# Storing each output tile with one transfer, and splitting the last tile's buffers, in a gated-attention + MLP kernel

## The chip, the cores and the metric

The kernel runs on one core of a Trainium2 chip. The metric is device time of one execution in microseconds (us). In three runs it took 189.67, 190.49 and 190.68 us; the median is 190.49 us.

## The reference

Two parts follow one another. The first is a gated linear recurrence over 768 positions for 4 batches of 8 heads, with a head size of 48; the state of a head is a 48x48 matrix:

```python
for t in range(S):
    state = alpha[:, :, t, :, None] * state + einsum('bhd,bhe->bhde', k[:, :, t], v[:, :, t])
    y[:, :, t] = einsum('bhd,bhde->bhe', q[:, :, t], state)
```

The second takes the heads of a position side by side as a row of 384 numbers, so that x has 4 x 768 = 3072 rows, and runs a two-layer network over them, with w_in of 384x2048 and w_out of 2048x384:

```python
h = x @ w_in
g = h * cos(h)
return (g @ w_out).astype(float32)
```

The output has 3072 rows of 384 float32, 4.72 MB in all.

## The kernel before

**Tiles.** The positions are worked off in 12 groups J of 256 (three to a batch). A group is held as pairs: a partition holds an even and an odd position beside one another in the inputs, so that a load of one input for one group (`load`, L105) brings 128 partitions x 8 heads x 384 bytes, 384 KB, and the group's output rows come out in two tiles c = 0 and 1 of 128 rows.

**Stages of a group.** `mul_a` and `ln` take logarithms of alpha, `cums` sums them on TensorE (PE), `icp` and `exps` turn them into decay factors on ScalarE (ACT), `scale_k` and `scale_q` (L212, L216) apply these to k and q, mostly on GpSimd (POOL). `trans`, `scores`, `mask` and `outer` build the attention inside the group, `add_state` and `decay_state` carry the state. `stack_v` (L225) copies v within the on-chip memory (SBUF) with four transfers of 64 partitions x 1 KB into the tile `vs`, and `yT` (L340) needs `vs` for its second set of matmuls. Then come the two layers: `mlp1` (L359, w_in), `cosine` (L365), `gate` (L370), and `mlp2` (L387, w_out), which sums a tile of outputs over 16 matmuls in a single bank of the accumulation memory (PSUM), tag "o". `evict_o` (L396) copies that bank to one of four SBUF tiles `o_sb`, and `store` (L403) writes it to the output in DRAM.

**The last tile.** For group 11, c = 1, `mlp2` puts the two halves of 192 columns in the two banks of one PSUM tile `o_last` (L381), `evict_o` copies one half with ACT and the other with VectorE (DVE) into the two halves of one `o_sb` tile (L394), and `store` writes each half with two transfers.

**Stores.** Row 2i+e of a tile's 128 output rows lies in partition 64e+i. `store` therefore writes the even and the odd rows with a transfer each: 64 partitions x 1536 bytes, to 64 rows that are 3072 bytes apart.

**Order.** It is written out by hand: `PLAN` gives each step of each group a number, the steps are recorded in the order of these numbers, and every engine and every queue works off its own steps in that order. All loads, all `stack_v` copies and nearly all stores are issued by one queue, that of the SyncE engine (SP); two stores of the last tile are issued by ACT's queue, the weights by POOL's. A transfer waits at the issuer for the work that it depends on, and all that is behind it in the queue waits with it. The framework also gives the SP and ACT transfers eight semaphores in turn, so that each waits for the landing of the one eight places ahead of it. Each `o_sb` buffer comes free when the store that reads it has landed.

In the SP queue, the order around the steps that matter here is, from 45 us on: eight tiles' stores, 28 loads and the `vs` copies of groups 3, 4, 6, 5 and 7; then further stores, the copies of groups 8 to 10 and the last load; and at the end the stores of (group, c) (8,1) and (7,0), the `vs` copy of group 11, and the stores (8,0), (9,0), (7,1), (10,0), (9,1), (10,1), (11,0) and (11,1).

Of the kernel before, what the change touches and what calls it, by code (L numbers as in the profile page):

```python
# [9 lines left out]
FP = mybir.dt.float32  # L10
# [6 lines left out]
def kernel(  # L17
# [10 lines left out]
    nc = tc.nc  # L28
    B, H, S, D = q.shape
    DM, DF = moe_w_in.shape  # L30
    C = 128
    HC = C // 2
    T2 = 2 * C
    NJB = S // T2
    NJ = B * NJB
# [12 lines left out]
    sb = ctx.enter_context(tc.tile_pool(name="sb", bufs=2))  # L48
    ps = ctx.enter_context(tc.tile_pool(name="ps", bufs=1, space=bass.MemoryType.PSUM))
# [30 lines left out]
    for lst, nm, n in ((lna_t, "lna", NL), (kh_t, "kh", NQ), (qh_t, "qh", NQ), (vp_t, "vp", NV)):  # L80
        for r in range(n):
            t = consts.tile([C, 2, H, 64], BF, tag=f"{nm}{r}", name=f"{nm}{r}")
            nc.vector.memset(t[:, :, :, D:64], 0.0)
            lst.append(t)
    for r in range(NS):
        t = consts.tile([C, 2, H, 64], BF, tag=f"vs{r}", name=f"vs{r}")
# [8 lines left out]
    w2 = consts.tile([C, NF, DM], BF, tag="w2", name="w2")  # L95

    a_sb, kqv, cp_sb, icp_sb, qkT_sb, A_sb, c2_sb = {}, {}, {}, {}, {}, {}, {}
    xT, gsb = {}, {}
# [72 lines left out]
    def two_banks(name):  # L171
        return ps.tile([C, 2, 512], FP, tag="h", name=name, bufs=3)
# [179 lines left out]
    h_ps, c_sb, o_ps, o_sb = {}, {}, {}, {}  # L352
# [20 lines left out]
    HALVES = [slice(0, DM // 2), slice(DM // 2, DM)]  # L373

    def mlp2(J, c, part):
        if (J, c) == (NJ - 1, 1):
            if part == 0:
                o_ps[J, c] = two_banks("o_last")
            for z, cols in enumerate(HALVES):
                for ft in range(part * NF // MP, (part + 1) * NF // MP):  # L380
                    nc.tensor.matmul(o_ps[J, c][:, z, 0 : DM // 2], gsb[J][:, ft, c * C : (c + 1) * C], w2[:, ft, cols],  # L381
                                     start=(ft == 0), stop=(ft == NF - 1))
            return
        if part == 0:
            o_ps[J, c] = ps.tile([C, 512], FP, tag="o", name="o_ps", bufs=1)
        for ft in range(part * NF // MP, (part + 1) * NF // MP):
            nc.tensor.matmul(o_ps[J, c][:, 0:DM], gsb[J][:, ft, c * C : (c + 1) * C], w2[:, ft],  # L387
                             start=(ft == 0), stop=(ft == NF - 1))

    def evict_o(J, c, copy):  # L390
        o_sb[J, c] = sb.tile([C, DM], FP, tag="o_sb", name="o_sb", bufs=4)
        if (J, c) == (NJ - 1, 1):
            for z, cp in enumerate((nc.scalar.copy, nc.vector.tensor_copy)):
                cp(out=o_sb[J, c][:, HALVES[z]], in_=o_ps[J, c][:, z, 0 : DM // 2])  # L394
        else:
            copy(out=o_sb[J, c], in_=o_ps.pop((J, c))[:, 0:DM])  # L396

    def store(J, c):
        rows = out[J * T2 + c * C : J * T2 + (c + 1) * C, :].rearrange("(i e) d -> e i d", e=2)
        for cols in HALVES if (J, c) == (NJ - 1, 1) else [slice(0, DM)]:  # L400
            for e in range(2):
                eng = nc.scalar if (J, c, e) == (NJ - 1, 1, 1) else nc.sync
                eng.dma_start(out=rows[e][:, cols], in_=o_sb[J, c][HC * e : HC * e + HC, cols])  # L403

    idle_ps = []

    def idle(n):
# [13 lines left out]
        "evT": lambda J, c, eng="DVE": evict_T(J, c, copies[eng]), "scores": scores, "mask": mask, "outer": outer,  # L421
        "add": add_state, "state": decay_state, "yT": yT, "evy": lambda J, c, eng="ACT": evict_y(J, c, copies[eng]),
        "m1": mlp1, "sin": cosine, "gate": gate, "m2": mlp2, "evo": lambda J, c, eng="ACT": evict_o(J, c, copies[eng]),
        "out": store, "idle": idle,
    }

# [70 lines left out]
    for key, line in PLAN.items():  # L497
        kind, *rest = key.split()
        for J, word in enumerate(line.split()):
            if word != "-":  # L500
                t, _, eng = word.partition(":")
# [38 lines left out]
```

## Time and profile before

| what | value |
|---|---|
| median of three runs | 190.49 us |
| the profiled execution's own time | 189.73 us |
| its span, first to last instruction | 187.7 us |
| PE busy | 177.2 us, 94% of the span |
| DVE, ACT, POOL busy | 134.3, 125.3, 77.4 us |
| read from DRAM, written to DRAM | 25.17 MB, 4.72 MB |
| transfers of SP's queue: loads, `vs` copies, stores | 48, 36, 48 |
| stores from ACT's queue | 2 |
| store of 96 KB, issue to landing (median) | 2.7 us |

The profile shows one execution. Busy time is the time in which an engine ran an instruction; a wait is put down to what came last. The shares of DMA are those of 16 DMA engines together, worked out from the times of the packets, which can overlap, so that a share can go over 1. Around the span the execution has 2.0 us that belong to no instruction.

### The profile page before, as it was taken

What the parts mean: (1) busy time and instruction counts of PE and PEld (TensorE: products, weight loads), DVE (VectorE), ACT (ScalarE), POOL (GpSimd) and SP (SyncE); (2) the same over time, 40 slices, a digit from 0 to 9 for tenths busy, and PEclk for the clock granted to TensorE, in tenths of its full rate; (3) what the DMA queues carried; (4) which work ended last, traced back from release to release, by engine and by line L of the source; (5) the groups of instructions that cost most, each with busy time, mean ns of one, the idle gap of its engine ahead of it and who ended that gap; (6) DMA issues with size and microseconds to landing.
All of it is one profiled execution on the core that took longest, in us unless ns stands there. A gap on an engine that the chain in (4) does not pass through costs nothing.

```text
span 187.7 us, 5795 instructions
## 1 busy us (share of the span) xinstructions
PE 177.2 (94%) x2471; PEld 126.7 (67%) x2474; DVE 134.3 (72%) x184; ACT 125.3 (67%) x161; POOL 77.4 (41%) x110
## 2 busy tenths in 40 slices
PE   7997799998999999999999999999999999999990
PEld 2444678664577776775688668686776786776880
DVE  7069775589799899589657986885876666573550
ACT  2466876899598977788577999728956182372520
POOL 5059610257664733783894068830540310100000
PEclk9999999999999999999999999999999999999998
DMA  6999999999959988996799943600042005501303
GB/s 152 261 256 154 185 203 236 255 264 265 249 137 302 265 184 217 265 268 166 195 280 259 216 106 90 166 0 3 3 114 73 0 21 124 128 1 45 84 0 84
DMA packets 60537, 29.47 MB, mean 157 GB/s; under 512 B 51424, under 2 KB 60512, under 8 KB 60512
## 3 DMA queue, kind: packets, MB, share of 16 engines
q1 hardware_dynamic: 56640, 25.86, 59.8%
q0 software_dynamic: 3712, 3.15, 11.0%
q8 instruction: 19, 0.31, 0.7%
q10 hardware_dynamic: 160, 0.10, 0.2%
q14 instruction: 6, 0.05, 0.1%
HBM read 25.17 MB, written 4.72 MB: 159 GB/s over the span
## 4 chain that ended last, share of the span: by engine, by line
PE 71%; ACT 16%; DVE 7%; issue 3%; DVEq 0%
PE h_ps L359 31%; PE o_ps L387 23%; PE idle_ps L411 5%; PE y_ps L340 3%; ACT c_sb L365 3%; ACT qkT L266 3%; DVE gsb L370 3%; PE T_ps L260 2%; ACT cp L200 2%; ACT L136 2%; ACT L365 2%; PE A_ps L274 2%; PE U_ps L291 2%; ACT lna L141 2%; ACT icp L192 2%
## 5 line engine op out<-in xcount | busy, mean ns | idle before, releaser
L370 DVE TENSOR_TENSOR gsb<-h_ps,c_sb 128x1024 bf16<-128x1024 f32 x48 | 58.1, 1221 | 22.3 <-ACT c_sb L365 21.5
L365 ACT ACTIVATE c_sb<-h_ps,halfpi 128x1024 bf16<-128x1024 f32 x48 | 53.0, 1113 | 27.4 <-PE h_ps L359 23.4
L359 PE MATMUL h_ps<-xT,w 128*128 128x256 bf16 x576 | 66.7, 273 | 1.4 <-issue 0.6
L387 PE MATMUL o_ps<-w,gsb 128*128 128x384 bf16 x368 | 66.7, 326 | 0.0
L359 PEld LDWEIGHTS <-w 128*128 128x128 bf16 x576 | 55.6, 98 | 10.4 <-issue 1.9
L387 PEld LDWEIGHTS <-gsb 128*128 128x128 bf16 x368 | 33.8, 98 | 21.2 <-DVE gsb L370 0.6
L313 POOL TENSOR_TENSOR un<-us,c 128x384 bf16<-128x384 f32 x20 | 16.8, 843 | 40.3 <-DVE us L305 33.9
L279 DVE TENSOR_TENSOR A_sb<-A_ps,msk 128x1024 bf16<-128x1024 f32 x24 | 28.9, 1216 | 1.3 <-PE A_ps L274 1.3
L212 POOL TENSOR_TENSOR kh<-k,icp 128x384 bf16<-128x384 f32 x17 | 16.9, 999 | 8.7 <-ACT icp L192 8.7
L216 POOL TENSOR_TENSOR qh<-q,cp 128x384 bf16<-128x384 f32 x15 | 15.4, 1032 | 10.9 <-ACT cp L200 10.9
L149 POOL TENSOR_TENSOR a<-a 128x384 f32<-128x384 f32 x9 | 9.3, 1037 | 12.9 <-DMA a<-in_alpha_dram 12.9
L411 PE MATMUL idle_ps<-zeros 128*128 128x512 bf16 x42 | 12.7, 445 | 1.6 <-DVE zeros L52 1.2
L219 POOL CAST vp<-v 128x768 bf16<-128x768 f32 x12 | 9.9, 824 | 9.0 <-DMA v<-in_v_dram 8.9
L141 ACT ACTIVATE lna<-a 128x768 bf16<-128x768 f32 x12 | 10.2, 846 | 4.5 <-DMA a<-in_alpha_dram 4.5
L136 ACT ACT_TABLE_LOAD x9 | 11.5, 1283 | 0.9 <-PEq L524 0.7
L266 ACT COPY qkT<-T_ps 128x1024 bf16<-128x1024 bf16 x8 | 8.0, 1016 | 6.2 <-PE T_ps L260 3.8
L266 DVE COPY qkT<-T_ps 128x1024 bf16<-128x1024 bf16 x16 | 10.8, 682 | 1.3 <-ACT qkT L266 1.3
L365 ACT ACT_TABLE_LOAD x9 | 11.5, 1283 | 0.2
L305 DVE TENSOR_TENSOR us<-U_ps,un 128x384 f32<-128x384 f32 x16 | 8.7, 550 | 3.8 <-PE U_ps L291 2.8
L396 DVE COPY o_sb<-o_ps 128x384 f32<-128x384 f32 x12 | 6.6, 552 | 6.6 <-PE o_ps L387 6.6
L274 PE MATMUL A_ps<-qkT 48*128 48x128 bf16 x192 | 9.2, 218 | 1.0 <-ACT vs L239 0.6
L396 ACT COPY o_sb<-o_ps 128x384 f32<-128x384 f32 x11 | 5.3, 478 | 7.1 <-PE o_ps L387 5.2
(69 smaller groups left out, 155.1 us busy)
## 6 DMA issues: line engine op xcount, KB each, us to landing
k<-in_k_dram SPq DMA_DIRECT2D x12, 384.0 KB, 5.5
a<-in_alpha_dram SPq DMA_DIRECT2D x12, 384.0 KB, 5.9
v<-in_v_dram SPq DMA_DIRECT2D x12, 384.0 KB, 6.2
q<-in_q_dram SPq DMA_DIRECT2D x12, 384.0 KB, 6.0
out_dram<-o_sb SPq DMA_DIRECT2D x46, 96.0 KB, 2.7
vs<-vp SPq DMA_DIRECT2D x36, 64.0 KB, 2.0
w<-in_moe_w_out_dram POOLq DMA_DIRECT2D x4, 384.0 KB, 9.9
w<-in_moe_w_in_dram POOLq DMA_DIRECT2D x4, 384.0 KB, 7.0
```

The source lines that it names most:

```text
L136: nc.scalar.preload_act_table_set("natural_log_exp_and_others")
L141: nc.scalar.activation(out=lna_t[J % NL][:, :, :, 0:D].rearrange("p e h d -> p h e d"), in_=a_sb.pop(J), func=AF.Ln)
L212: eng.tensor_tensor(out=kh_t[J % NQ][:, e, :, 0:D], in0=kqv["k", J][:, :, e], in1=icp_, op=ALU.mult)
L216: eng.tensor_tensor(out=qh_t[J % NQ][:, e, :, 0:D], in0=kqv["q", J][:, :, e], in1=cp, op=ALU.mult)
L266: copy(out=qkT_sb[J][:, c], in_=T_ps[J][:, c].rearrange("r n e s -> r n (e s)"))
L279: nc.vector.tensor_tensor(out=A_sb[J][:, c].rearrange("s a p t -> s (a p) t"), in0=A_ps.pop((J, c)).rearrange("s a p t -> s (a p) t"), in1 ...
L313: nc.gpsimd.tensor_tensor(out=u, in0=U_sum.pop(n), in1=c2_sb[J][:, :, c].unsqueeze(3).to_broadcast([C, NP, 2, D]), op=ALU.mult)
L359: nc.tensor.matmul(h_ps[J, u][:, f, :], w1[:, kk, ft * C : (ft + 1) * C], xT[J][:, kk, :], start=(kk == 0), stop=(kk == KT - 1))
L365: nc.scalar.activation(out=c_sb[J, u], in_=h_ps[J, u], func=AF.Sin, bias=halfpi, scale=1.0)
L370: nc.vector.tensor_tensor(out=gsb[J][:, u * FW : (u + 1) * FW], in0=h_ps.pop((J, u)), in1=c_sb.pop((J, u)), op=ALU.mult)
L387: nc.tensor.matmul(o_ps[J, c][:, 0:DM], gsb[J][:, ft, c * C : (c + 1) * C], w2[:, ft], start=(ft == 0), stop=(ft == NF - 1))
L411: nc.tensor.matmul(idle_ps[0], zeros[:, 0:C], zeros, start=True, stop=True)
```

## The change

Three things change. The last tile's halves get a PSUM tile each (tag "x", which the cumulative sums used before, and one bank of tag "h") and an SBUF tile each. Each tile of outputs is stored by one transfer, of which the destination is written as 2 x 64 rows x 384 columns (e, i, d) and the source as 128 partitions x 384. Of the last tile's two transfers, 2 x 64 x 192 each, ACT issues the first and SP the second. The number of stores goes from 50 to 25 (24 on SP, one on ACT); the order of the steps on the engines stays.

```diff
     def mlp2(J, c, part):
         if (J, c) == (NJ - 1, 1):
             if part == 0:
-                o_ps[J, c] = two_banks("o_last")
+                o_ps[J, c] = [ps.tile([C, 512], FP, tag="x", name="o_last", bufs=1), two_banks("o_last")[:, 0]]
             for z, cols in enumerate(HALVES):
                 for ft in range(part * NF // MP, (part + 1) * NF // MP):
-                    nc.tensor.matmul(o_ps[J, c][:, z, 0 : DM // 2], gsb[J][:, ft, c * C : (c + 1) * C], w2[:, ft, cols],
+                    nc.tensor.matmul(o_ps[J, c][z][:, 0 : DM // 2], gsb[J][:, ft, c * C : (c + 1) * C], w2[:, ft, cols],
                                      start=(ft == 0), stop=(ft == NF - 1))
             return
...
     def evict_o(J, c, copy):
-        o_sb[J, c] = sb.tile([C, DM], FP, tag="o_sb", name="o_sb", bufs=4)
         if (J, c) == (NJ - 1, 1):
+            o_sb[J, c] = []
             for z, cp in enumerate((nc.scalar.copy, nc.vector.tensor_copy)):
-                cp(out=o_sb[J, c][:, HALVES[z]], in_=o_ps[J, c][:, z, 0 : DM // 2])
+                t = sb.tile([C, DM // 2], FP, tag=f"o_half{z}", name="o_half", bufs=1)
+                cp(out=t, in_=o_ps[J, c][z][:, 0 : DM // 2])
+                o_sb[J, c].append((t, HALVES[z], (nc.scalar, nc.sync)[z]))
         else:
-            copy(out=o_sb[J, c], in_=o_ps.pop((J, c))[:, 0:DM])
+            t = sb.tile([C, DM], FP, tag="o_sb", name="o_sb", bufs=4)
+            copy(out=t, in_=o_ps.pop((J, c))[:, 0:DM])
+            o_sb[J, c] = [(t, slice(0, DM), nc.sync)]

     def store(J, c):
         rows = out[J * T2 + c * C : J * T2 + (c + 1) * C, :].rearrange("(i e) d -> e i d", e=2)
-        for cols in HALVES if (J, c) == (NJ - 1, 1) else [slice(0, DM)]:
-            for e in range(2):
-                eng = nc.scalar if (J, c, e) == (NJ - 1, 1, 1) else nc.sync
-                eng.dma_start(out=rows[e][:, cols], in_=o_sb[J, c][HC * e : HC * e + HC, cols])
+        for t, cols, eng in o_sb.pop((J, c)):
+            eng.dma_start(out=rows[:, :, cols], in_=t)
```

## The prediction

> **What bounds the kernel now.** I read the page first: PE is busy for 94% of the span, and the chain that ended last is mostly PE (71%). So a store can cost time in two ways only: it makes PE wait (through a late load, a late `vs` copy or an `o_sb` buffer that isn't free), or it lands late at the very end. From the page:
>
> ```profile
> span 187.7 us, 5795 instructions
> PE 177.2 (94%) x2471; PEld 126.7 (67%) x2474; DVE 134.3 (72%) x184; ACT 125.3 (67%) x161; POOL 77.4 (41%) x110
> ...
> DMA  6999999999959988996799943600042005501303
> ...
> q1 hardware_dynamic: 56640, 25.86, 59.8%
> ...
> q10 hardware_dynamic: 160, 0.10, 0.2%
> ...
> out_dram<-o_sb SPq DMA_DIRECT2D x46, 96.0 KB, 2.7
> ```
>
> Two things are to be seen. The DMA engines are full or nearly so until about 110 us, with SP's queue (q1) carrying almost all. And the packet counts tell how transfers are shared: q10 is ACT's two stores of 64 rows, 128 packets, and 32 more, 16 to a transfer. q1 comes out the same way: 48 x (1024+16) loads + 48 x (64+16) stores + 36 x (64+16) copies = 56,640. Every transfer now ends with 16 marks, one for each of 16 engines; the trace's landing records, 16 to a transfer, say so too.
>
> Then the DMA view of the stretch that matters, 45.1 to 109 us:
>
> ```profile
> q<-in_q_dram SPq DMA_DIRECT2D x8, 384.0 KB, 5.8
> v<-in_v_dram SPq DMA_DIRECT2D x8, 384.0 KB, 6.1
> k<-in_k_dram SPq DMA_DIRECT2D x7, 384.0 KB, 5.2
> a<-in_alpha_dram SPq DMA_DIRECT2D x5, 384.0 KB, 5.4
> out_dram<-o_sb SPq DMA_DIRECT2D x17, 96.0 KB, 3.8
> vs<-vp SPq DMA_DIRECT2D x20, 64.0 KB, 2.8
> ```
>
> 28 loads, 8 tiles' stores (and a half of a ninth) and five groups of `vs` copies go through one queue. What an engine of the 16 pays for them comes from busy time by stretch (the last two columns are DMA share and GB/s):
>
> ```profile
> 62.00:68.00 6.00, 5.98 (x61) 4.85 (x59) 4.80 (x8) 5.89 (x8) 5.43 (x6) 1.00 1.20 263
> 139.00:142.00 3.00, 3.00 (x58) 2.25 (x57) 2.43 (x2) 1.32 (x3) 0.00 (x0) 1.00 0.62 152
> 173.50:173.70 0.20, 0.20 (x3) 0.10 (x1) 0.20 (x1) 0.00 (x0) 0.00 (x0) 1.00 0.06 23
> ```
>
> At 62 to 68 us there are loads alone: 393,216 bytes at 263 GB/s are 1.5 us per load. At 139 to 142 us stores alone, many engines busy: 152/(0.62 x 16) = 15.3 GB/s per busy engine, so a packet of 1536 bytes takes 100 ns. At 173.5 us the rest of one store, one engine busy: 23/(0.06 x 16) = 24 GB/s, 64 ns.
>
> Last, the timeline, for who needs what when:
>
> ```profile
> 105.89 2.47 SPq L225 DMA_DIRECT2D vs<-vp  x4
> ...
> 112.87 0.62 PE L340 MATMUL y_ps<-A_sb,vs 128*32 128x128 bf16 x32
> ...
> 153.37 2.39 SPq L403 DMA_DIRECT2D out_dram<-o_sb  x4
> 155.87 2.45 SPq L225 DMA_DIRECT2D vs<-vp  x4
> ...
> 183.48 0.32 ACT L394 COPY o_sb<-o_last 128x192 f32<-128x192 f32 x1 [4.21 <-PE o_last L381]
> ...
> 183.84 0.36 DVE L394 COPY o_sb<-o_last 128x192 f32<-128x192 f32 x1 [1.11 <-ACT o_sb L394]
> ```
>
> **The last tile's own buffers.** DVE's copy waits for ACT's now (1.11 us idle, ended by ACT); on its own tile it would start with PE's end, 183.48, 0.36 us earlier. The first half's sum ends four matmuls before the second's (16 take 1.48 us), so ACT could start 0.37 us earlier. Worth 0.2 to 0.4 us if the stores follow at once, and nothing if they don't (below). The bank of tag "x" was last read by the sums of group 11, by 133.4 us, so no wait there.
>
> **The store.** Removed: 25 transfers, at some 0.6 us of SP's time each, 14 us; SP is no bound and its transfers mostly wait for data, so I take 0 (cover gone, 0.6 us at the end). Added: a form that no row shows. All transfers of the trace have 64 or 128 as their first dimension, on both sides, and are shared by 16 engines. The new destination has 2 there. Bounds: 16 shares still, 8 packets each, 0.5 to 0.8 us a store; or 2 shares, 64 packets each, 64 x 64 ns = 4.1 us to 64 x 100 ns = 6.4 us a store, all on the same two engines. I take two shares, since the count of the first dimension is what all sixteen-share rows have in common and the one thing that differs in the new form. I take 64 ns, because the row nearest to two busy engines is the one with one busy engine.
>
> The Trainium skill, page "DMA: Bandwidth & Descriptors", section "Rules for kernel authors", says that an outermost dimension smaller than 16 confines the transfer to that many engines at most; by it the sum is the one below. The trace agrees as far as it goes (16 marks for 64 and 128) and shows no smaller size.
>
> **Middle, 45 to 113 us.** The two engines work off the queue in its order. The load of alpha issued at 43.1 us, the last ahead of the first store, lands at 49.5 us in the trace. From there to the `vs` copy of group 7: 8 stores x 4.1 = 32.8 us; 28 loads x 1.5 = 42.0; 5 copies x 16 packets of 1 KB, 43 to 67 ns each by the same two rates, 0.9 us a group, 4.5. Sum 79.3, so that copy lands at 128.8 us; `yT` of group 7 reads it at 112.87. PE stands for **15.9 us** there or ahead of it: `yT` of groups 3 to 6 meet parts of the same lag earlier, and these aren't added again. Bounds: loads at 24 GB/s as well (24.6 KB per engine, 1.0 us) give 32.8+28+3.5, 113.8 us, 0.9 us late; stores at 6.4 us give 51.2+42+5.4, 148.1, 35 us late. Once PE is late, what it releases later is issued later, and this is why the lag isn't counted again behind group 7: the copy of group 8, two places on, would land at 134 and is read at 128.8+15.9.
>
> **Buffers.** At 140.8 us (time of before) ACT's copy of tile (7,1) waits for the `o_sb` buffer of (5,1), whose store is issued at 138 and lands at 140.7. With 4.1 us it lands at 138+1.5+4.1 = 143.6 (1.5 us from issue to the first packet: 1.9 to 2.2 us to landing, less 0.4 us of packets). PE's next w_out matmuls start at 142.2 and would wait until the copy of 0.48 us is done, 144.1: **1.9 us** (0 to 4.2 us with the price).
>
> **End, from 153.4 us** (again time of before). Nine full stores 36.9 us, the copy of group 11 0.9, the two halves 2 x 64 x 32 ns = 4.1 us: 41.9 us of work for the two engines, from 153.4+1.5. The queue never runs empty (at 170.9 it reaches 176.3). Last landing 196.8, against 184.6+2.1 = 186.7 now: **10.1 us**; with 6.4 us a store 33 us. The 0.2 to 0.4 us of the last tile's buffers lie under this.
>
> Sum: 15.9+1.9+10.1 = 27.9 us on the profiled execution's 189.7 us (span 187.7 and 2.0 around it): 217.6, and since the median lies 0.8 us above that execution, **218 us**. From 0.9+0+9.7 on the low side, 200; with 6.4 us everywhere, 35+4+33, 262.
>
> **Rivals.** *Sixteen shares (not slower).* If the rows are dealt out whatever the first dimension, each engine writes 8 packets per store and nothing in the middle moves. DVE's copy ends at 183.84, SP issues 0.4 us later as now, and the landing takes 2.1+0.2 us: 186.5 against 186.7, **189.5 us**. For it: 1024 rows of a load are dealt out evenly as well. Against: these have 128 first. It decides from about four shares on: then a store is 2.05 us, the middle sums to 62.9 us, the copy lands at 112.4, in time. The Trainium skill, page "DMA: Bandwidth & Descriptors", section "Rules for kernel authors", also advises one 128-partition transfer in place of two of disjoint halves, which speaks for this case; the trace has no such pair to compare.
>
> *Two shares, but the middle hides them.* With loads near 1.0 us when only two engines are behind, the lag at group 7 is 1 to 4 us and only the end is left: **200 to 204 us**. For it: packets of loads overlap (share 1.20). Against: 263 GB/s is what they reach in every full stretch.
>
> *Two shares at the crowded price* of 100 ns: 240 to **262 us**. Against: the price was measured with most engines busy at once.
>
> **Chances.** Forecast (205 to 240 us) 0.64; middle hidden 0.12; crowded price 0.10; sixteen shares 0.13; anything else 0.01. The first three, 0.86, are slower, and so is the last: 0.87. Of the sixteen-share case I give 0.10 to no change and 0.03 to faster; 0.5%, 1 us, is what a measurement can tell here. The range 199 to 245 leaves out the sixteen shares and half of the crowded price, 0.18; the forecast's own range is 205 to 240.
>
> **What would show it.** Packets of q1: 48 x 1040 + 36 x 80 + 24 x (128+marks): 55,920 with two marks, 56,256 with sixteen; q10 130 or 144. Store landing at a median over 6 us instead of 2.7; loads over 8 us. `yT` waiting for `vs` copies near 130 us, PE below 85%, GB/s under 150 in slices that had 260, and stores landing 8 us or more after PE's last matmul. Sixteen marks in the landing records would make all of it wrong; two marks with PE never waiting in the middle would make the first 16 us wrong.

## The result and the profile after

The changed kernel takes 216.63 us (median of 6 runs, 216.11 to 217.56) against 190.59 us (6 runs, 189.64 to 190.78): the ratio is 1.139, with a 95% interval of 1.136 to 1.142. It is 26 us slower. The profiled execution took 216.11 us, with a span of 214.3 us, 26.6 us over the span of before.

From the page of the changed kernel:

```profile
span 214.3 us, 5758 instructions
PE 182.9 (85%) x2474; PEld 129.0 (60%) x2474; DVE 135.3 (63%) x184; ACT 125.7 (59%) x161; POOL 78.6 (37%) x110
...
PEclk9999999999999999859999999999979999999975
DMA  6999999994687967966947554101110042111110
...
q1 hardware_dynamic: 55920, 25.86, 49.3%
...
q10 hardware_dynamic: 130, 0.10, 0.1%
...
PE 57%; DMA 18%; ACT 5%; DVE 5%; SPq 4%; issue 3%; POOL 2%; DVEq 0%; POOLq 0%; ACTq 0%
```

q1 has the 55,920 packets that the prediction gave for two marks to a store, and q10 has 128 + 2. The DMA engines, all 16 together, are no longer full in most slices after some 48 us, and yet DMA has 18% of the chain that ended last, where it had none before. From busy time by stretch (last columns: granted clock, DMA share, GB/s), a stretch at the end in which only stores are left:

```profile
203.00:209.00 6.00, 0.00 (x0) 0.00 (x0) 0.00 (x0) 0.00 (x0) 0.00 (x0) 0.74 0.13 50
```

A share of 0.13 of 16 engines is 2.1 engines, and they move 50 GB/s, 24 GB/s each: 64 ns for a packet of 1536 bytes. The trace's records of packets of 1536 bytes have 65 ns as the 10th, 50th and 90th percentile, and in this stretch two of them begin every 61 ns, which is one on each of two engines; before it was 65 to 119 ns (10th and 90th) with a median of 104. So two engines carry every store, at the price that one engine alone had before.

The timeline shows where this reaches PE. The rows are of POOL, PE, ACT, DVE and SP, in order of time:

```profile
84.16 0.83 POOL L219 CAST vp<-v 128x768 bf16<-128x768 f32 x1 [7.25 <-DMA v<-in_v_dram]
...
89.03 0.38 PE L260 MATMUL T_ps<-ident_bf,kh 64*128 64x64 bf16 x14 [2.82 <-POOL kh L212]
...
125.07 0.88 PE L340 MATMUL y_ps<-A_sb,vs 128*32 128x128 bf16 x32 [2.70 <-DMA vs<-vp]
...
156.61 0.48 ACT L400 COPY o_sb<-o_ps 128x384 f32<-128x384 f32 x1 [5.46 <-DMA out_dram<-o_sb]
...
157.14 3.09 PE L388 MATMUL o_ps<-w,gsb 128*128 128x384 bf16 x12 [2.98 <-ACT o_sb L400]
...
177.54 0.56 DVE L400 COPY o_sb<-o_ps 128x384 f32<-128x384 f32 x1 [3.54 <-DMA out_dram<-o_sb]
...
202.03 0.51 SPq L406 DMA_DIRECT2D out_dram<-o_half  x1
```

A load of v is late for POOL, and through POOL's products for PE; the `vs` copy of group 7 is late for PE itself; two copies out of PSUM wait for a store to free their buffer; and the last store, issued at 202.0 us, is not down until 213.3.

How late PE is against before, at the start of the matmuls of `yT` that read `vs`:

| group | 3 | 4 | 5, 6 | 7 | 8 | 9 | 10 | 11 | end of PE | last landing |
|---|---|---|---|---|---|---|---|---|---|---|
| before, us | 60.1 | 74.9 | 93.5 | 112.9 | 128.7 | 144.2 | 155.4 | 167.0 | 183.45 | 186.7 |
| after, late by us | 0.2 | 2.4 | 9.8 | 12.2 | 12.0 | 16.2 | 16.7 | 18.2 | 18.2 | 26.5 |

The loss has three parts: 12.0 us up to group 8, 6.2 us from there to group 11, and 8.4 us between the end of PE and the last landing.

### The profile page after: what moved, and what is told of

Same layout as the page of the kernel before. It is cut to its first block, busy times and chain, and to the rows that moved or that the text cites. A ratio compares the mean times of both kernels' runs of the same rounds, so it can differ in the third digit from the quotient of the medians.

```text
span 214.3 us, 5758 instructions
## 1 busy us (share of the span) xinstructions
PE 182.9 (85%) x2474; PEld 129.0 (60%) x2474; DVE 135.3 (63%) x184; ACT 125.7 (59%) x161; POOL 78.6 (37%) x110
## 3 DMA queue, kind: packets, MB, share of 16 engines
q1 hardware_dynamic: 55920, 25.86, 49.3%
## 4 chain that ended last, share of the span: by engine, by line
PE 57%; DMA 18%; ACT 5%; DVE 5%; SPq 4%; issue 3%; POOL 2%; DVEq 0%; POOLq 0%; ACTq 0%
PE h_ps L359 21%; PE o_ps L388 20%; DMA out_dram<-o_sb 6%; DMA q<-in_q_dram 5%; DMA v<-in_v_dram 4%; PE idle_ps L414 4%; PE y_ps L340 3%; DMA vs<-vp 2%; PE A_ps L274 2%; SPq L225 2%; PE T_ps L260 2%; SPq L406 2%; DVE gsb L370 1%; ACT qkT L266 1%; PE U_ps L291 1%
## 5 line engine op out<-in xcount | busy, mean ns | idle before, releaser
L388 PE MATMUL o_ps<-w,gsb 128*128 128x384 bf16 x368 | 69.6, 337 | 4.3 <-ACT o_sb L400 3.0
L388 PEld LDWEIGHTS <-gsb 128*128 128x128 bf16 x368 | 34.6, 100 | 27.4 <-issue 7.4
L313 POOL TENSOR_TENSOR un<-us,c 128x384 bf16<-128x384 f32 x20 | 16.7, 835 | 48.8 <-DVE us L305 38.2
L216 POOL TENSOR_TENSOR qh<-q,cp 128x384 bf16<-128x384 f32 x15 | 16.1, 1078 | 13.2 <-ACT cp L200 10.7
L219 POOL CAST vp<-v 128x768 bf16<-128x768 f32 x12 | 10.1, 842 | 15.3 <-DMA v<-in_v_dram 15.3
L350 DVE CAST xT<-y_ps 128x384 bf16<-128x384 f32 x12 | 6.5, 553 | 8.1 <-PE y_ps L340 6.0
```

The lines of the kernel that those rows point to most:

```text
L216: eng.tensor_tensor(out=qh_t[J % NQ][:, e, :, 0:D], in0=kqv["q", J][:, :, e], in1=cp, op=ALU.mult)
L313: nc.gpsimd.tensor_tensor(out=u, in0=U_sum.pop(n), in1=c2_sb[J][:, :, c].unsqueeze(3).to_broadcast([C, NP, 2, D]), op=ALU.mult)
```

## The experiments

The theory: the loss comes from the first dimension of the store's destination, 2, because only two engines share the transfer, and all that stands behind it in the queue waits for these two. The rivals: that a big transfer is slow in itself, that the last tile's new buffers cost something, or that only one of the parts counts.

### The parts of the change alone

The first kernel has the last tile's own buffers, with every store in two transfers:

```diff
         for t, cols, eng in o_sb.pop((J, c)):
-            eng.dma_start(out=rows[:, :, cols], in_=t)
+            for e in range(2):
+                q_ = nc.scalar if (J, c, e) == (NJ - 1, 1, 1) else nc.sync
+                q_.dma_start(out=rows[e][:, cols], in_=t[HC * e : HC * e + HC])
```

> Only the last tile's two halves get PSUM and SBUF tiles of their own; every store keeps its two transfers of 64 rows. If the time of the change comes from the stores (theory of shares), this is 0.2 to 0.4 us under before (190.1 to 190.4 us), since both copies start earlier and the stores follow at once. If the new buffers cost something themselves (rival: a bank that comes free late), it lies 1 us or more over before.

190.01 us against 190.08, ratio 0.999 (0.997 to 1.001). The buffers cost nothing that can be measured, and gain nothing that can: 0.07 us, where 0.2 to 0.4 had been expected. In the trace both copies do start earlier against the end of PE's work (DVE's 0.04 us behind it instead of 0.39, bound by PE and no longer by ACT), but each half still is two transfers, which follow one another at the issuer, and the last landing comes 3.1 us behind PE's end instead of 3.3.

The second has the old last tile and one transfer of 2 x 64 rows for all other tiles:

```diff
+        if (J, c) != (NJ - 1, 1):
+            nc.sync.dma_start(out=rows, in_=o_sb[J, c])
+            return
-        for cols in HALVES if (J, c) == (NJ - 1, 1) else [slice(0, DM)]:
+        for cols in HALVES:
```

> Only the stores: one transfer of 2 x 64 rows for every tile but the last, whose buffers and four transfers stay as before. Theory of shares: all but the last halves' own work on the two engines stays, 210.2 to 212.9 us in the trace of after, so 213 to 214 us. Rival that the last tile's new buffers carry a good part: under 205 us.

213.29 us, ratio 1.121 (1.116 to 1.125). The form of these stores is 23 us of the 26. The 3 us that are missing fit the work of the last two halves on the two engines (2.7 us in the trace of after, from 210.2 to 212.9), but only roughly: PE's end is 1.4 us later in this run's trace than after the change, and its tail, from PE's end to the last landing, 3.5 us shorter.

### The number of engines

If a partition's row number is changed, the destination gets another first dimension with the same bytes and the same single transfer. The copy of `evict_y` reorders the columns of a tile while it copies them; for n = 4:

```diff
-        copy(out=xT[J][:, :, c * C : (c + 1) * C], in_=y_ps[J][:, c, 0 : KT * C].rearrange("r (i t) -> r i t", i=KT))
+        copy(out=xT[J][:, :, c * C : (c + 1) * C].rearrange("r i (m s) -> r i m s", m=2),
+             in_=y_ps[J][:, c, 0 : KT * C].rearrange("r (i s m) -> r i m s", i=KT, m=2))
...
-        rows = out[J * T2 + c * C : J * T2 + (c + 1) * C, :].rearrange("(i e) d -> e i d", e=2)
+        rows = out[J * T2 + c * C : J * T2 + (c + 1) * C, :].rearrange("(i e) d -> e i d", e=4)
```

For n = 8 and 16, m is 4 and 8 and e is n. In the last variant row and partition have the same number, and the destination is just 128 x 384:

```diff
+        copy(out=xT[J][:, :, c * C : (c + 1) * C].rearrange("r i (s e) -> r i s e", e=2),
+             in_=y_ps[J][:, c, 0 : KT * C].rearrange("r (i e s) -> r i s e", i=KT, e=2))
...
-        rows = out[J * T2 + c * C : J * T2 + (c + 1) * C, :].rearrange("(i e) d -> e i d", e=2)
+        rows = out[J * T2 + c * C : J * T2 + (c + 1) * C, :]
...
-            eng.dma_start(out=rows[:, :, cols], in_=t)
+            eng.dma_start(out=rows[:, cols], in_=t)
```

> The changed kernel, with the columns of a tile reordered in the copy after the attention so that the destination is 4 x 32 rows instead of 2 x 64: still one transfer per tile, same bytes and packets. Theory of shares: four engines, 32 packets of 65 ns, 2.1 us a store; the middle then has 49.5 + 8 x 2.1 + 28 x 1.4 + 4, 109.5 us, in time for 112.9, and at the end the last landing is 182.8 + 1.5 + 2.1 + 2 x 1.2 = 188.8 us, 2 us late: 192 to 193 us, marks of 4 for each store. Rival that one big transfer is slow whatever its form: 214 to 218 us.

> The changed kernel, with the columns reordered so that a partition holds the row of its own number: the destination is then 128 x 384 and still one transfer per tile. Theory of shares: 16 engines, 8 packets each, 0.5 us a store, no lag in the middle and none at the end: 189.5 to 190.8 us, if the reordered copies (24 of 0.48 to 0.56 us) keep their length. Rival that one big transfer is slow whatever its form: 214 to 218 us.

> As the kernel with four shares, but with a destination of 8 x 16 rows: eight marks to a store and 16 packets of 65 ns for an engine, 1.05 us. Four shares lost 7.8 us, of which 3.2 to 3.5 at group 7, 1.5 in the buffers and 2.9 at the end. With half the work per engine the load of v that was 2.8 us late is 0.5 us late at most and the end 0.5 to 1 us: 190 to 192 us. If the loss goes with the form (more than one dimension of rows) and not with the number of engines, it stays at 196 to 198 us.

> The destination as 16 x 8 rows, one transfer per tile: 16 marks and 8 packets per engine, as with 128 rows in order, but with two dimensions of rows. If the number of engines is all that counts, 188.7 to 189.5 us, the time of the rows in order. If two dimensions of rows cost something themselves, 190 us or more.

| first dimension | marks per store, from q10 | time, us | ratio to before (95%) |
|---|---|---|---|
| 2 (the change) | 2 | 216.63 | 1.139 (1.136 to 1.142) |
| 4 | 4 | 197.96 | 1.043 (1.038 to 1.047) |
| 8 | 8 | 191.39 | 1.005 (1.002 to 1.007) |
| 16 | 16 | 189.62 | 0.997 (0.995 to 0.998) |
| 128 | 16 | 189.01 | 0.994 (0.992 to 0.997) |

Each ratio is to the time of before that was measured with that run. The queue rows of ACT's one store of 128 rows, from the pages of the kernels with 4, 8 and 128 first (with 16 it is 144 too):

```profile
q10 hardware_dynamic: 132, 0.10, 0.1%
```

```profile
q10 hardware_dynamic: 136, 0.10, 0.2%
```

```profile
q10 hardware_dynamic: 144, 0.10, 0.2%
```

The marks go with the first dimension, and the time with the marks. One transfer of 192 KB isn't slow in itself: with 16 engines it beats the two transfers of before. The reordered copies are no part of this: in all of these kernels they take the 0.55 us on DVE and 0.48 us on ACT of before. With 16 x 8 rows the time lies between what was expected of the two theories, and whether two dimensions of rows cost something (16 against 128) isn't settled; the intervals overlap, and the two were compared with before on different chips. The traces point to the end: from PE's end to the last landing it is 2.7 us with 16 x 8 rows and 2.0 with 128.

Four shares took 5 us more than I had expected, and this shows what the working had left out. From the timeline of POOL, first before, then with four shares:

```profile
76.08 0.83 POOL L219 CAST vp<-v 128x768 bf16<-128x768 f32 x1 [1.67 <-DMA v<-in_v_dram]
```

```profile
78.89 0.83 POOL L219 CAST vp<-v 128x768 bf16<-128x768 f32 x1 [4.52 <-DMA v<-in_v_dram]
```

POOL already waited for this load of v before the change: it had no slack at all. With four shares it lands 2.8 us later, and PE is 3.5 us late at groups 5 and 6, and still 3.2 at group 7, though the `vs` copy of group 7 is in time. I had looked for lateness only at the copies of v. Of these 3.5 us PE stands only a part: behind the wait its granted clock is 0.64 from 86 to 88 us and 0.50 from 88 to 90, which by an estimate from these two numbers loses 1.7 us (see the last section). From there to PE's end the lag grows by another 1.7 us, most of it at group 9, where ACT's copy of tile (7,1) waits 3.6 us for a store, and the end adds 2.9.

The kernel with rows in order is the version that beats both: 189.01 us against 190.08, 1.1 us or 0.6% under before. Its end, from the timeline:

```profile
184.37 0.32 ACT L397 COPY o_half<-o_last 128x192 f32<-128x192 f32 x1 [3.87 <-PE o_last L383]
184.70 0.36 DVE L397 COPY o_half<-o_last 128x192 f32<-128x192 f32 x1 [0.76 <-PE o_last L383]
184.72 0.36 ACTq L407 DMA_DIRECT2D out_dram<-o_half  x1
185.09 0.33 SPq L407 DMA_DIRECT2D out_dram<-o_half  x1
```

SP issues right behind DVE's copy, and the last landing comes 2.0 us after PE's end (184.7 to 186.7), where it came 3.3 us after it before (183.4 to 186.7). This 1.3 us fits the gain of 1.1 in the medians (the profiled execution itself, 189.60 us, was only 0.1 us faster than that of before, as PE ended 1.2 us later in it). The likely cause is one issue per half instead of two; no run tests it by itself. The trace of the first experiment has the same early copies and 3.1 us from PE's end to the last landing, so the buffers alone don't bring it.

### The parts of the loss

Only the tiles with number 2J+c under 11 by one transfer of 2 x 64, the others by two of 64:

```diff
+            if 2 * J + c < 11:
+                eng.dma_start(out=rows[:, :, cols], in_=t)
+                continue
+            for e in range(2):
+                q_ = nc.scalar if (J, c, e) == (NJ - 1, 1, 1) else nc.sync
+                q_.dma_start(out=rows[e][:, cols], in_=t[HC * e : HC * e + HC])
```

> The changed kernel, but only the first 11 tiles by number (groups 0 to 4 and tile (5,0), stored by 119 us in the trace of before) go out by one transfer of 2 x 64 rows; the later ones keep two transfers of 64. If the parts of the prediction add up, this has the lag of the middle alone, 12.2 us at group 7 in the trace of after, and no late landings: 201 to 203 us. Rival that the end alone carries the loss: under 195 us.

And the reverse, with `>= 11`:

> The reverse: the first 11 tiles keep two transfers of 64 rows, the later ones and the last halves go out by one transfer of 2 x 64. If the parts add up: the buffer waits behind group 8 (12.0 to 18.1, 6 us) and the late landings at the end (8.4 us) alone, 190.1 + 14.4, 203 to 206 us; with the loss of the kernel before it sums with the early stores' to the whole 26 us. Rival that the middle alone carries the loss: under 195 us.

203.29 and 203.91 us against 190.46: +12.8 and +13.4 us (the first a little over what was expected), together 26.3, the whole loss of 26.0. In the first trace PE's lag at groups 4, 5/6, 7 and 8 is 2.4, 8.9, 12.0 and 13.3 us, and then stays; in the second there is none up to group 8, 4.7 at group 9 and 6.2 at the end of PE, and the last landing is 15.0 us late. So the parts add, and neither hides behind the other.

Eight buffers for output tiles in the changed kernel (`bufs=4` to `bufs=8`):

> The changed kernel with eight instead of four buffers for output tiles, so that the copies out of PSUM needn't wait for a store to land. If the steps behind group 8 come from these buffers (waits of 5.5 us on ACT and 3.5 us on DVE), 4 to 6 us go: 210 to 213 us, with no wait of a copy for a store left. If they come from something else, 216 to 217 us.

213.6 us (three of the four runs 211.2 to 213.6, the fourth 215.9), ratio 1.118 (1.110 to 1.126): 3 us less, where 4 to 6 had been expected. No copy out of PSUM waits for a store any more, and PE's lag stays at 14.2 us from group 8 to the end instead of climbing from 12.0 to 18.2. So the 6.2 us behind group 8 do come from the buffers. That the kernel gains less has two reasons in the trace: at group 8 PE is 2.2 us later than after the change, as its clock was 0.50 for 6 us behind the wait at group 7 (see the last section), and the end takes 1.5 us more: the last landing comes 9.9 us later behind PE's end than before, instead of 8.4. More buffers take the waits away, but not the work of the two engines that are full.

One step of the order moved in the changed kernel, the store of tile (1,1) behind two more loads:

```diff
-        "out 1": "44770 66136 87674 100827 112274 133721 136121 156752 149522 168228 170958 180161",
+        "out 1": "44770 68100 87674 100827 112274 133721 136121 156752 149522 168228 170958 180161",
```

> The changed kernel with one step of the order moved: the store of tile (1,1) stands two loads later in SP's queue, behind the load of v for group 6, on which POOL waits 7.3 us in the trace of after. If a transfer waits for the work of the two engines that is ahead of it in the queue, that v lands 4 us sooner (at 80 us instead of 84), PE's lag at groups 5 and 6 falls from 9.8 to about 6 us, and the lag at group 7 stays, as the work ahead of its vs copy is the same: 216 to 217 us again, at best 215. If the lag of groups 5 and 6 is what sets the rest, 212 to 213 us.

216.45 us. From its timeline, POOL and PE:

```profile
80.17 0.83 POOL L219 CAST vp<-v 128x768 bf16<-128x768 f32 x1 [3.25 <-DMA v<-in_v_dram]
```

```profile
124.27 1.21 PE L340 MATMUL y_ps<-A_sb,vs 128*32 128x128 bf16 x32 [4.68 <-DMA vs<-vp]
```

The v is there 4.0 us sooner, the price of one store, and PE's lag at groups 5 and 6 is 5.5 us instead of 9.8. But at group 7 it is 11.4 us again (12.2 after the change): PE now waits 4.7 us for the copy instead of 2.7, since the same work is ahead of it. This bears out how the prediction sums for group 7: what counts there is the amount of work in the queue ahead, not its order.

## Why the prediction was right

218 us was forecast, 216.6 measured, and the case was the one that was given 0.64. The mechanism is the one forecast: two engines carry each store, what stands behind it in the queue waits for them, and PE and the end are late by that. But the total came closer than its parts, and this was luck: up to group 8 the forecast has 15.9 us and the runs 12.0, for the buffers 1.9 and 6.2, for the end 10.1 and 8.4. A term that was 3.9 us too big and one that was 4.3 us too small nearly cancel. By its steps:

- **Two shares.** Shown by the marks and by the five first dimensions. The other side of it, sixteen shares, was put at 189.5 us, which is 0.2 us under the profiled execution of before (the 0.8 us up to the median, which the 218 us have, weren't added there); the runs gained 0.5 us with 16 x 8 rows and 1.1 with 128 in order. The point from which the sharing decides was put too low: four shares were to save the middle, but they cost 7.9 us, and eight still cost 0.9. The step that failed there is that only the copies of group 7 were held against the queue; the load of v, on which POOL already waited, has no slack and takes any delay.
- **The price.** 64 ns a packet from the row with one engine busy; 65 measured. So the crowded price of 100 ns doesn't hold here.
- **The middle.** 15.9 us forecast, 12.2 measured at group 7. Two terms were too big, the loads (28 x 1.5 us) by 2.6 us and the stores by 1.6. A packet of 384 bytes takes 22 ns now (the median of all; the records don't say which engine), 64 of them 1.4 us, and stores take 64 x 61 ns, 3.9 us: 49.5 + 31.2 + 39.4 + 4.5 = 124.6 us, and PE starts on that copy at 125.07. The second rival, that the middle hides the two shares, was wrong.
- **The lag of groups 3 to 6** was called a part of the same, and it is the same two engines, but by another way: at groups 5 and 6 it was the load of v and POOL, not the `vs` copies, and PE's clock of 0.50 behind that wait.
- **The buffers.** 1.9 us forecast for tile (7,1), whose copy did wait 5.5 us; PE stood for 3.0 us there, and the lag grew by 4.2 us. Two things were missing. Behind this stand PE's clock was 0.53 and 0.62 for 4 us: the sum has no term for the clock anywhere, see below. And the copy at 177.5 us waited for the store of tile (8,1) (3.5 us), of which the prediction says nothing; this is the 1.5 us between groups 10 and 11.
- **The end.** 10.1 us forecast, 8.4 measured. While PE waits for a buffer, the two engines work on: without these waits, with eight buffers, the end is 9.9 us late. The sum of buffers and end is 14.6 us against 12.0. That the last tile's own buffers are worth nothing under the late stores held.

## What to carry to other kernels

Two transfers aren't cheaper as one when the one has a small dimension first: count the landing marks per transfer, or the packets over the rows, and give the destination a first dimension that keeps all 16 engines. Here 16 and 128 did; 2, 4 and 8 didn't. Other numbers, and another first dimension at the source, weren't tried. A total DMA share that is low says nothing about two engines of the 16 that are full; the sign is loads and copies that land late while the share falls. Before a transfer is made longer, look in the view of waits for engines that already wait on a load behind it: they have no slack.

## What the runs showed of the hardware that I had not expected

The clock that is granted to PE can fall after PE has stood, and this makes a wait cost more than its length. From busy time by stretch of the changed kernel (PE's busy time comes first, then its weight loads, DVE, ACT and POOL; then the granted clock):

```profile
86.00:88.00 2.00, 0.20 (x2) 0.09 (x2) 0.11 (x1) 0.00 (x0) 2.00 (x4) 1.00 1.19 280
88.00:90.00 2.00, 0.38 (x14) 0.26 (x14) 0.00 (x0) 0.00 (x0) 2.00 (x4) 0.96 1.23 266
90.00:92.00 2.00, 1.23 (x19) 0.81 (x20) 0.00 (x0) 0.58 (x1) 1.84 (x3) 0.50 0.94 198
92.00:94.00 2.00, 2.00 (x8) 0.99 (x7) 1.54 (x2) 1.97 (x3) 0.00 (x0) 0.50 0.76 209
94.00:96.00 2.00, 2.00 (x21) 1.04 (x20) 0.84 (x2) 2.00 (x5) 0.87 (x1) 0.50 0.49 131
...
154.00:156.00 2.00, 0.16 (x2) 0.00 (x0) 0.01 (x1) 0.00 (x0) 0.00 (x0) 1.00 0.13 50
156.00:158.00 2.00, 0.86 (x6) 0.54 (x6) 0.00 (x0) 1.39 (x3) 0.00 (x0) 1.00 0.13 51
158.00:160.00 2.00, 2.00 (x8) 0.80 (x6) 1.65 (x2) 1.01 (x1) 0.00 (x0) 0.53 0.13 50
160.00:162.00 2.00, 2.00 (x49) 1.42 (x48) 0.27 (x1) 0.42 (x2) 0.00 (x0) 0.62 0.17 58
```

From 86 to 90 us PE is busy for 0.58 us, and from 90 to 96 its clock is 0.50; it stands 3.0 us at 154 us, and has 0.53 and 0.62 from 158 to 162. An estimate from these rows: 5.23 us of work at 0.50 and 2 us each at 0.53 and 0.62 lose 2.6 + 0.9 + 0.8, 4.3 us, and PE's busy time as a whole rose by 5.7 us (177.2 to 182.9). Before the change every stretch of 2 us up to PE's end had a clock of 1.00. The Trainium skill, page "TensorE: Matmul & The Clock Gate", section "Why this matters for your kernels", says that idle gaps of over about 3 us bring the clock down to half; the trace agrees with the half, and here a gap of 3.0 us was enough.

The length of a gap alone doesn't decide it. At group 7 after the change PE stood for 2.70 us (the row at 125.07 above), and its clock stayed at 1.00. With the early stores alone it stood for 2.50 us at the same place, and its clock fell to 0.50. First the stretch of the changed kernel, then the wait and the same stretch of the other:

```profile
126.00:128.00 2.00, 2.00 (x47) 1.79 (x44) 2.00 (x4) 0.03 (x1) 2.00 (x4) 1.00 0.56 143
```

```profile
124.83 0.85 PE L340 MATMUL y_ps<-A_sb,vs 128*32 128x128 bf16 x32 [2.50 <-DMA vs<-vp]
...
126.00:128.00 2.00, 2.00 (x30) 1.47 (x25) 2.00 (x5) 0.00 (x0) 2.00 (x4) 0.50 0.59 160
```

From group 7 to 8 the lag falls by 0.2 us in the first and grows by 1.4 in the second. What decides between the two, these runs don't show.

A store of 128 rows in one dimension takes SP 0.33 us to issue, one of 2, 4, 8 or 16 groups of rows 0.51 to 0.60 us (the last halves of each kernel), so the form of a transfer also shows at the issuer.
